# A causal attention with two expert layers behind it: joint transposes of the first keys, PReLU split between ScalarE and VectorE, low words in place

## The chip, the cores and the metric

The kernel runs on one core of a Trainium2 chip. The metric is the device time of one execution in microseconds (us). The kernel before takes 504.18 us (median of three runs, 503.7 to 505.47).

## What is computed

Everything is float32. A causal attention over 2 batches, 12 heads, 448 positions and 64 values a head, then two expert layers on its 896 x 768 output:

```python
scores = q @ k.T / 8; scores above the diagonal = -1e9
attn   = softmax(scores)                # exp(s - max), divided by (sum + 1e-9)
x      = (attn @ v)                     # heads side by side: 896 x 768
h      = x @ w_in                       # 768 -> 2048
y      = (max(h, 0) + alpha * min(h, 0)) @ w_out          # PReLU, 2048 -> 768
m      = max(max(y @ w1, y @ w2), y @ w3)                 # 768 -> 768
out    = m @ w_out2                     # 768 -> 768
```

## The kernel before

**Three products for one.** The expert layers multiply in a rounded 32-bit type. To keep float32's accuracy each operand is split into a high and a low part (`h`, `l`), and `product` (L403) issues three matmuls: high by high, low by high, high by low. All of them carry line 406: 2004 of the program's 2684 matmul records lie behind the attention.

**The weights arrive as 64-bit floats.** Class `Weights` (L301) loads 128 columns at a time as pairs of 32-bit words (`raw`) and makes float32 of them: ScalarE takes the size from the high word into `t` (`size`, L369) and scales the low word into a tile of its own, `r` (`low`, L387); VectorE clamps and shifts `t` (L373, L376), puts in the sign (`top`, L390) and adds `r` as integers (`both`, L401; a few on GpSimd); ScalarE then rounds the high part `wh` (L281) and VectorE or GpSimd subtracts for the low part `wl` (L293). `raw` has two buffers and is free again after `top`.

**Attention.** Twelve jobs, each of two heads (j = 0, 1) that share a batch. The 448 query rows are cut into four chunks c of 64, 128, 128 and 128 rows; chunk c sees 64, 192, 320 or 448 keys. A job runs: scores on TensorE (`ps`, L578) in two groups, chunks 3 and 0 and then 2 and 1; the mask and the row minimum of the negated scores on VectorE (L595); exponential and row sum on ScalarE (L608); the sums' reciprocals on VectorE (L619, L620); normalising on GpSimd (L624); transposes of the result on TensorE (`pt`, L643) in three banks a head: the first 64 keys (four transposes), keys of blocks 1 and 3 (four), keys of block 2 (two); a copy of each bank to SBUF (`p`, on VectorE or ScalarE, L287, L281); the product with v (`pv`, L652), the two heads in the two column halves of the array; and the split of its result into `xh` and `xl`.

**Order.** A planner (class `Plan`, L71) gives every step a rank, an estimated duration and a list of what must precede it, and writes out each engine's instructions in the order in which its own estimate would start them. Every engine then runs its list in order. While the attention runs, products of the first expert layer for the first batch's tokens (five blocks of 128 outputs, `NB`, ranks from `FILL_RANK`) are set between the attention's matmuls: they are called fillers here. 48 of their matmuls stand ahead of the last `pv`, 42 behind it.

**PReLU.** `prelu` (L670): VectorE takes alpha times the negative part from PSUM (L676), adds the positive part, also from PSUM (L686); ScalarE rounds the high part `g_h` (L281), VectorE subtracts for `g_l` (L293). The PSUM bank is free after the second VectorE instruction. Behind the attention seven banks serve these products.

**Start.** Eight matmuls on a tile of zeros (`warm`, L714) keep TensorE busy until the first q and k are there. The zeros are written by VectorE (L259).

Of the kernel before, what the change touches and what calls it, by code (L numbers as in the profile page):

```python
# [23 lines left out]
RINGS = dict(w=4, m=1, s=4, t=3, v=4, qk=3, e=3, p=4)  # L24
NB = 5
HELD = 4
WARM = 8
# [3 lines left out]
    load=-6, s=12, max=12, exp=16, recip=10,  # L31
# [6 lines left out]
FIRST = 0  # L38
SLACK = 0.02
# [31 lines left out]
class Plan:  # L71
# [27 lines left out]
    def add(  # L99
        self, rank, engines, fn, after=(), take=(), give=(), delay=0.0, port=False, mode="full"  # L100
    ):
# [6 lines left out]
        self.waiting[i] = (rank, engines, fn, after, tuple(take), give, delay, port, mode)  # L108
        self.open[i] = sum(d in self.waiting for d in after)
        for d in after:  # L110
            self.next.setdefault(d, []).append(i)
        if not self.open[i]:
            self.ready[i] = None
        return i

    def start(self, step):
# [12 lines left out]
        for engine, took in engines.items():  # L129
# [6 lines left out]
            if engine == "PE" and mode != self.mode:  # L136
# [9 lines left out]
    def run(self):  # L146
        while self.waiting:
# [20 lines left out]
            if engine == "PE":  # L168
                self.mode = mode
# [18 lines left out]
def attention_moe_moe2_kernel(  # L188
# [73 lines left out]
    mask = first.tile([P, S], F32, name="mask")  # L262
    nc.gpsimd.memset(mask, 0.0)
    nc.gpsimd.affine_select(
        out=mask[:, S - P :],
        in_=mask[:, S - P :],
        compare_op=ALU.is_ge,
        fill=FILL,
        base=0,
        pattern=[[-1, P]],  # L270
        channel_multiplier=1,
    )
    alpha_sb = const.tile([P, KF], F32, name="alpha_sb")
    nc.scalar.dma_start(out=alpha_sb, in_=alpha)
# [26 lines left out]
    class Weights:  # L301
# [3 lines left out]
        def __init__(self, rank, w, k0, n, f, parts=None, lo_engines=("DVE", "POOL"), after=()):  # L305
# [19 lines left out]
                rank, on_act(k, words=True), step(self.low), (load,), take=("cr",)  # L325
            )
            top = plan.add(
                rank, on_dve(k), step(self.top), (high, low), give=(("raw", load),), port=True
            )
            both = plan.add(  # L330
                rank, on_dve(k) | on_pool(k), self.both, (top, low), give=(("cr", low),), port=True
# [76 lines left out]
    class Product:  # L408


        def __init__(self, rank, pieces, bank, token):

            total = len(pieces)
            self.end = None
            for i, (count, n, terms, after, give) in enumerate(pieces):
                self.end = plan.add(
                    rank,
# [19 lines left out]
    BANKS = ((0,), (1, 3), (2,))  # L437
    AT_COL, BANK_COL = {}, [0]
# [7 lines left out]

    p_all = [at.tile([P, BANK_COL[-1]], F32, bufs=1, name=f"p{i}") for i in range(RINGS["p"])]
    for p in p_all:
        nc.vector.memset(p[ROWS[0] :, : BANK_COL[1]], 0.0)
# [4 lines left out]
    e_all = [at.tile([P, 2, NP], F32, bufs=1, name=f"e{i}") for i in range(RINGS["e"])]  # L454
    for e in e_all:
        nc.vector.memset(e[ROWS[0] :, :, : OFF[1]], 0.0)
    used = {"p": 0, "e": 0}
# [5 lines left out]
    class Job:  # L463


        def __init__(self, rank, b, hp):
            self.b, self.hp = b, hp
            self.ps, self.pt, self.p = {}, {}, {}

            def add(kind, *args, **kw):  # L470
# [3 lines left out]
            load_v = add("load", on_dma(256), step(self.load_v), take=("v",), delay=1.8)  # L474

            norm = [[], []]
            s = None
            for i, cs in enumerate(PAIRS):
# [7 lines left out]
                    give=(("qk", load_qk),) * (i == len(PAIRS) - 1),  # L486
# [21 lines left out]
                for c in cs:  # L508
                    for j in range(2):
                        took = on_pool(START[c + 1], two=False)  # L510
                        if b * HP + hp < FIRST:
                            took |= on_dve(START[c + 1], fast=True)
                        norm[j].append(
                            add("norm", took, partial(self.normalize, i, c, j), (r,), port=True)
# [3 lines left out]
            for j in range(2):  # L518
                for n in range(len(BANKS)):
                    w = BANK_COL[n + 1] - BANK_COL[n]  # L520
                    keys = sum(ROWS[kc] for kc in BANKS[n] for c in range(kc, NCH))
                    t = add(
                        "p",
                        {"PE": keys * 0.85e-3 + 0.03},
                        step(self.p_t, j, n),
                        norm[j] if t is None else [*norm[j], t],
                        take=("t",) + ("p",) * (n == 0),
                        give=(("e", e_took),) * (j == 1 and n == len(BANKS) - 1),
                    )
                    if n == 0:  # L530
                        p_took.append(t)
                    src = partial(self.pt.get, (j, n))
                    outs.append(
                        add(
                            "p_out",
                            on_dve(w, psum=True) | on_act(w, psum=True),
                            copy(partial(self.p_part, j, n), src),
                            (t,),
                            give=(("t", t),),
                        )  # L540
                    )
            a = add(
                "av",
                {"PE": 4 * BANK_COL[-1] / 2400},
# [3 lines left out]
                mode="columns",  # L548
# [464 lines left out]
```

## Time and profile before

| | |
|---|---|
| median of three runs | 504.18 us |
| the profiled execution | 504.13 us |
| its span, first to last instruction | 502.3 us |
| TensorE busy (PE) | 495.1 us, 99% |
| VectorE, ScalarE, GpSimd busy | 360.6, 256.9, 63.5 us |
| attention, to the last `pv` | 101.0 us |
| the rest, line 406 without a gap | 397.9 us |

In the profile PE is TensorE's matmuls, PEld its weight loads, DVE VectorE, ACT ScalarE, POOL GpSimd. A matmul record overlaps the next one, so its own duration says little: what one costs is the distance from its start to the next start. The granted TensorE clock is 1.00 (2.4 GHz) in every stretch shown below. A matmul in plain float32 (`ps`, `pv`) leaves two records, so 16 records of `pv` are the eight matmuls of one job.

### The profile page before, as it was taken

The page shows a single profiled execution, that of the slowest core. Times are in us where ns is not written, and L with a number is a line of the kernel's source. Part 1 is how long each engine was busy: PE and PEld are TensorE (multiplying, and loading weights), DVE is VectorE, ACT ScalarE, POOL GpSimd, SP SyncE. Part 2 cuts the span into 40 slices and gives each one's busy share as a digit, 9 for nine tenths or more (in the row PEclk, how much of TensorE's full clock was granted, in tenths as well). Part 3 has the DMA queues.
Part 4 walks back from the last instruction along what each step waited for, and adds up shares of the span by engine and source line. Part 5 has one row for each costly group of instructions (what it writes and reads, how often), then busy time and mean ns, then how long its engine had stood idle before and what let it go on. Part 6 is the DMA issues. An engine that isn't in the chain of part 4 may idle for free.

```text
span 502.3 us, 7218 instructions
## 1 busy us (share of the span) xinstructions
PE 495.1 (99%) x2684; PEld 427.5 (85%) x2684; DVE 360.6 (72%) x727; ACT 256.9 (51%) x502; POOL 63.5 (13%) x113
## 2 busy tenths in 40 slices
PE   8999999999999999999999999999999999999997
PEld 5665666789989899898899899898899899889997
DVE  7889878859999999968557467579999896601000
ACT  5999898645453555434425335366566544401111
POOL 3657755330100000000000000000000000000000
PEclk9999999999999999999999999999999999999999
DMA  7635410213332333333333343253554443000111
GB/s 255 234 88 173 154 44 13 111 67 125 127 126 78 112 127 105 116 115 106 115 116 104 93 138 122 69 185 128 188 186 160 157 134 118 1 1 31 64 64 63
DMA packets 14147, 56.70 MB, mean 113 GB/s; under 512 B 1696, under 2 KB 3488, under 8 KB 14112
## 3 DMA queue, kind: packets, MB, share of 16 engines
q1 hardware_dynamic: 13968, 56.24, 33.7%
q8 instruction: 21, 0.34, 0.3%
q14 instruction: 14, 0.11, 0.1%
q10 hardware_dynamic: 144, 0.01, 0.0%
HBM read 53.49 MB, written 2.75 MB: 112 GB/s over the span
## 4 chain that ended last, share of the span: by engine, by line
PE 94%; DVE 3%; ACT 2%; issue 0%; DVEq 0%
PE ps L406 81%; PE pt L643 4%; PE pv L652 4%; PE ps L578 4%; DVE e L595 2%; ACT e L608 1%; DVE sm L619 1%; PE warm L714 1%; DVE p L287 0%; ACT p L281 0%; DVE sm L620 0%; ACT o L281 0%; DVE nm L595 0%; ACT xh L281 0%; DVE zeros L259 0%
## 5 line engine op out<-in xcount | busy, mean ns | idle before, releaser
L406 PE MATMUL ps<-xh,wh 128*128 128x384 f32 (+2 forms) x408 | 149.4, 366 | 0.0
L406 PE MATMUL ps<-xh,wl 128*128 128x384 f32 (+2 forms) x408 | 148.7, 364 | 0.0
L406 PE MATMUL ps<-xl,wh 128*128 128x384 f32 (+2 forms) x408 | 148.5, 364 | 0.0
L406 PEld LDWEIGHTS ps<-xh,wh 128*128 128x128 f32 x408 | 76.7, 188 | 8.4 <-DVE xl L293 0.3
L406 PEld LDWEIGHTS ps<-xl,wh 128*128 128x128 f32 x408 | 76.6, 188 | 8.1
L406 PEld LDWEIGHTS ps<-xh,wl 128*128 128x128 f32 x408 | 76.5, 188 | 7.8
L281 ACT CAST wh<-t 128x768 fp32r<-128x768 f32 (+1 forms) x53 | 43.0, 811 | 73.3 <-DVE t L401 73.0
L406 PE MATMUL ps<-g_h,wl 128*128 128x512 f32 (+1 forms) x192 | 70.0, 365 | 0.0
L406 PE MATMUL ps<-g_l,wh 128*128 128x512 f32 (+1 forms) x192 | 69.9, 364 | 0.0
L406 PE MATMUL ps<-g_h,wh 128*128 128x512 f32 (+1 forms) x192 | 69.6, 362 | 0.0
L369 ACT ACTIVATE t<-raw 128x768 f32<-128x768 f32 (+1 forms) x59 | 52.3, 887 | 14.0 <-DMA raw<-in_moe_w_dram 5.0
L293 DVE TENSOR_TENSOR wl<-t,wh 128x768 fp32r<-128x768 f32 (+1 forms) x47 | 43.3, 921 | 21.9 <-ACT wh L281 21.9
L390 DVE SCALAR_TENSOR_TENSOR t<-raw,t 128x768 uint32<-128x768 uint32 (+1 forms) x59 | 54.7, 927 | 0.9
L401 DVE CUSTOM_DVE_ANT_0 t<-t,r 128x1536 uint16<-128x1536 uint16 (+1 forms) x57 | 52.6, 924 | 2.2
L387 ACT ACTIVATE r<-raw 128x768 uint32<-128x768 uint32 (+1 forms) x59 | 52.0, 881 | 4.1 <-DMA raw<-in_moe_w_dram 3.1
L608 ACT ACTIVATE e<-e,nm 128x448 f32<-128x448 f32 (+3 forms) x96 | 47.8, 503 | 5.1 <-DVE nm L595 4.9
L624 POOL TENSOR_SCALAR e<-e,sm 128x448 f32<-128x448 f32 (+3 forms) x96 | 45.6, 494 | 31.2 <-DVE sm L620 12.5
L406 PEld LDWEIGHTS ps<-g_l,wh 128*128 128x128 f32 x192 | 36.0, 188 | 4.1
L406 PEld LDWEIGHTS ps<-g_h,wh 128*128 128x128 f32 x192 | 36.1, 188 | 4.1
L406 PEld LDWEIGHTS ps<-g_h,wl 128*128 128x128 f32 x192 | 36.0, 188 | 3.8
L281 ACT CAST g_h<-g 128x512 fp32r<-128x512 f32 (+2 forms) x32 | 18.1, 567 | 39.2 <-DVE g L686 39.0
L595 DVE CUSTOM_DVE_ANT_0 e<-ps,mask 128x448 f32<-128x448 f32 (+3 forms) x96 | 35.2, 413 | 4.1 <-PE ps L578 3.9
(53 smaller groups left out, 584.0 us busy)
## 6 DMA issues: line engine op xcount, KB each, us to landing
raw<-in_moe_w_dram SPq DMA_DIRECT2D x18, 768.0 KB, 4.3
raw<-in_moe_w_in_dram SPq DMA_DIRECT2D x17, 768.0 KB, 4.4
raw<-in_moe_w_out_dram SPq DMA_DIRECT2D x12, 768.0 KB, 4.4
raw<-in_moe_w_out_dram SPq DMA_DIRECT2D x12, 640.0 KB, 4.1
qk<-in_qk_dram SPq DMA_DIRECT2D x12, 448.0 KB, 3.5
v<-in_v_dram SPq DMA_DIRECT2D x12, 256.0 KB, 2.7
out_dram<-o SPq DMA_DIRECT2D x14, 192.0 KB, 1.9
alpha_sb<-in_moe_alpha_dram ACTq DMA_DIRECT2D x1, 8.0 KB, 3.5
```

The lines of the kernel that those rows point to most:

```text
L281: nc.scalar.copy(out(), src())
L293: ENGINE[engine].tensor_tensor(out=out(), in0=a(), in1=f32(b()), op=ALU.subtract)
L369: nc.scalar.activation(out=f32(self.t), in_=f32(self.raw[..., 1]), func=AF.Abs)
L387: nc.scalar.activation(out=self.r, in_=self.raw[..., 0], func=AF.Copy, scale=2.0**-29)
L390: nc.vector.scalar_tensor_tensor(out=self.t, in0=self.raw[..., 1], scalar=0xC0000000, in1=self.t, op0=ALU.bitwise_and, op1=ALU.bitwise_or,)
L401: ENGINE[engine].tensor_tensor(out=t, in0=t, in1=self.r.bitcast(I32), op=ALU.add)
L406: nc.tensor.matmul(ps, a, c, start=(first and y == 0), stop=(last and y == 2))
L578: nc.tensor.matmul(ps, self.qk[d, 0, START[c] : START[c] + P], self.qk[d, 1, :n], start=True, stop=True,)
L595: nc.vector.tensor_tensor_reduce(out=self.e_part(c, j), in0=self.ps[c, j], in1=mask[: ROWS[c], m - n : m], op0=ALU.add, op1=ALU.min, scale ...
L608: nc.scalar.activation(out=s, in_=s, func=AF.Exp, scale=-1.0, bias=self.column(self.nm, i, c, j), accum_out=self.column(self.sm, i, c, j),)
L624: ENGINE[engine].tensor_scalar(out=s, in0=s, scalar1=self.column(self.sm, i, c, j), scalar2=1.0, op0=ALU.mult, op1=ALU.mult,)
L643: nc.tensor.transpose(pt[:keys, o : o + P], self.e[:, j, s : s + keys], ident)
```

## The change

1. **Joint transposes.** Head 0's keys are reversed on the host, so that its first 64 keys stand last in each row of the probabilities, right ahead of head 1's first 64 keys. One 128 x 128 transpose then covers both heads' first keys. v's first rows are laid out as one 128 x 128 block, zero where a row belongs to the other head, so the first matmul of `pv` takes both heads at once on the whole array, and six on column halves follow. Banks per job go from six to five: key block 2 (two transposes) and key blocks 1 and 3 (four) for each head, then the joint one (four), which is last and needs both heads.
2. **First job.** Its scores come in three groups, chunks 1 and 0, then 2, then 3.
3. **PReLU behind the attention.** ScalarE reads the PSUM bank twice, relu(-h) into `n` and relu(h) into `g`; VectorE joins them, `g - alpha * n`. The bank is free after ScalarE's second reading; `n` has one buffer. The five products of the early tokens keep the old form.
4. **Low words in place.** ScalarE writes the scaled low words over the raw low words; the integer addition reads them there, every second word; `raw` is free after the addition.
5. **Order behind the attention.** The two token blocks (512 and 384) alternate: each weight block begins with the token block that the one before it ended with, and the pieces of w_out are taken weight by weight.
6. **Small.** Nine warming matmuls on a constant instead of eight on zeros; two masks; alpha is loaded by SyncE instead of ScalarE's queue, and VectorE negates it once; four memsets of `p` are gone.

```diff
-RINGS = dict(w=4, m=1, s=4, t=3, v=4, qk=3, e=3, p=4)
+RINGS = dict(w=4, m=1, s=4, t=3, v=4, qk=3, e=3, p0=2, p=4)
-WARM = 8
+WARM = 9
-    plan.buffers(**RINGS, raw=2, ct=2, cr=2, eg=2)
-    zeros = first.tile([P, S], mybir.dt.bfloat16, name="zeros")
-    nc.vector.memset(zeros, 0.0)
+    plan.buffers(**RINGS, raw=2, ct=2, eg=2, en=EN)
+    ones = nc.const_aps.tensor(1.0, [P, S], mybir.dt.bfloat16)
...
         def low(self):
-            self.r = wcvt.tile([P, KC, P], U32, tag="r", name="r")[:, : self.n]
-            nc.scalar.activation(out=self.r, in_=self.raw[..., 0], func=AF.Copy, scale=2.0**-29)
+            low = self.raw[..., 0]
+            nc.scalar.activation(out=low, in_=low, func=AF.Copy, scale=2.0**-29)
...
-            ENGINE[engine].tensor_tensor(out=t, in0=t, in1=self.r.bitcast(I32), op=ALU.add)
+            ENGINE[engine].tensor_tensor(out=t, in0=t, in1=self.raw[..., 0].bitcast(I32), op=ALU.add)
...
-    BANKS = ((0,), (1, 3), (2,))
+    BANKS = ((2,), (1, 3))
...
+            self.groups = ((1, 0), (2,), (3,)) if rank == 0 else PAIRS
...
-            for j in range(2):
-                for n in range(len(BANKS)):
+            parts = [(j, kcs) for j in range(2) for kcs in BANKS] + [(0, (0,))]
+            for j, kcs in parts:
...
-                    s = OFF[c] + START[kc]
-                    o = AT_COL[kc] - BANK_COL[n] + START[c] - START[kc]
-                    nc.tensor.transpose(pt[:keys, o : o + P], self.e[:, j, s : s + keys], ident)
+                    o = AT_COL[kc] - AT_COL[kcs[0]] + START[c] - START[kc]
+                    s = 2 * OFF[c] + START[c + 1] + (START[kc] if j else -START[kc + 1])
+                    nc.tensor.transpose(pt[:, o : o + P], self.e[:, s : s + P], ident)
...
-            for kc in range(NCH):
+            nc.tensor.matmul(
+                pv, self.v[:, 0].rearrange("p j d -> p (j d)"), self.p0, start=True, stop=False
+            )
+            for kc in range(1, NCH):
...
+        def parts():
+            o["n"] = epi.tile([P, BANK], F32, tag="n", bufs=EN, name="n")[:, :N]
+            o["g"] = epi.tile([P, BANK], F32, tag="g", name="g")[:, :N]
+            nc.scalar.activation(out=o["n"], in_=prod.ps[:, :N], func=AF.Relu, scale=-1.0)
+            nc.scalar.activation(out=o["g"], in_=prod.ps[:, :N], func=AF.Relu)
+        def join():
+            nc.vector.scalar_tensor_tensor(
+                out=o["g"], in0=o["n"], scalar=minus_alpha[:, f : f + 1], in1=o["g"],
+                op0=ALU.mult, op1=ALU.add,
+            )
```

Where the instructions stand now. On TensorE, the first job's scores and transposes in the kernel before (`ps` scores, `pt` transposes; x2 means twice in a row):

```order
17 L578 MATMUL ps<-qk 128x448 x2
18 L578 MATMUL ps<-qk 128x64 x2
19 L578 MATMUL ps<-qk 128x320 x2
20 L578 MATMUL ps<-qk 128x192 x2
...
27 L578 MATMUL ps<-qk 128x320 x2
28 L578 MATMUL ps<-qk 128x192 x2
29 L643 MATMUL pt<-ident,e_126 64x128 x4
30 L643 MATMUL pt<-ident,e_126 128x128 x6
31 L643 MATMUL pt<-ident,e_126 64x128 x4
32 L643 MATMUL pt<-ident,e_126 128x128 x6
33 L578 MATMUL ps<-qk 128x448 x2
```

and now:

```order
19 L612 MATMUL ps<-qk 128x192 x2
20 L612 MATMUL ps<-qk 128x64 x2
21 L612 MATMUL ps<-qk 128x320 x2
22 L612 MATMUL ps<-qk 128x448 x4
...
26 L612 MATMUL ps<-qk 128x448 x2
27 L612 MATMUL ps<-qk 128x64 x2
28 L681 MATMUL pt<-ident,e_121 128x128 x6
29 L612 MATMUL ps<-qk 128x320 x2
30 L612 MATMUL ps<-qk 128x192 x2
31 L681 MATMUL pt<-ident,e_121 128x128 x10
```

The first group has 256 columns a head instead of 512, and the first job issues 16 transposes (6 and 10) where it issued 20; the first six stand ahead of the third job's second group of scores. On TensorE, a product with v and what stands around it in the kernel before (fourth job):

```order
86 L578 MATMUL ps<-qk 128x448 x2
87 L578 MATMUL ps<-qk 128x64 x2
88 L652 MATMUL pv<-p_113,v 64x448
89 L652 MATMUL pv<-p_115,v 64x448
90 L652 MATMUL pv<-p_113,v 64x384
```

and now (fourth job):

```order
70 L612 MATMUL ps<-qk 128x448 x2
71 L612 MATMUL ps<-qk 128x64 x2
72 L691 MATMUL pv<-p_571,v 128x448
73 L696 MATMUL pv<-p,v 64x384 x2
74 L696 MATMUL pv<-p,v 64x256 x2
75 L696 MATMUL pv<-p,v 64x128 x2
76 L681 MATMUL pt<-ident,e_122 128x128 x4
```

Seven matmuls instead of eight; the first fills the whole array, so the change to column halves falls inside the product. On ScalarE, in the stage of w_in, the kernel before has

```order
183 L369 ACTIVATE t<-raw 128x768
184 L387 ACTIVATE r<-raw 128x768
185 L281 CAST g_h<-g 128x512
186 L281 CAST g_h<-g 128x384
187 L281 CAST wh<-t 128x768
```

and the same stretch now:

```order
218 L399 ACTIVATE t<-raw 128x768
219 L417 ACTIVATE raw<-raw 128x768
220 L311 CAST g_h<-g 128x512
221 L737 ACTIVATE n<-ps 128x512
222 L738 ACTIVATE g<-ps 128x512
223 L311 CAST g_h<-g 128x384
224 L311 CAST wh<-t 128x768
225 L737 ACTIVATE n<-ps 128x384
226 L738 ACTIVATE g<-ps 128x384
```

ScalarE has five instructions for a weight block before and nine now. Up to the last `pv` the TensorE list holds 240 transposes and 48 fillers before, 192 and 30 now; the numbers of matmuls on line 406 over the whole program are the same.

## Rows read from the trace of the kernel before

**Rows 1.** Page: busy us by engine.
```profile
PE 495.1 (99%) x2684; PEld 427.5 (85%) x2684; DVE 360.6 (72%) x727; ACT 256.9 (51%) x502; POOL 63.5 (13%) x113
```
**Rows 2.** The closing chain in order of time: start us, us, what.
```profile
1.15 3.17 PE warm L714 x8
4.32 1.77 PE ps L578 x8
...
101.03 397.94 PE ps L406 x2004
```
**Rows 3.** Timeline of PE, one job's turn: start us, us, instruction, records.
```profile
28.75 2.43 PE L643 MATMUL pt<-ident,e 128*128 128x128 f32 x20
31.11 1.19 PE L578 MATMUL ps<-qk 64*128 64x448 f32 x8
32.23 2.27 PE L652 MATMUL pv<-p,v 128*64 128x448 f32 x16
34.43 0.44 PE L643 MATMUL pt<-ident,e 128*128 128x128 f32 x2
34.79 1.13 PE L578 MATMUL ps<-qk 64*128 64x320 f32 x8
35.86 1.73 PE L643 MATMUL pt<-ident,e 128*64 128x128 f32 x14
```
**Rows 4.** Stretches of 0.05 us, the product with v alone: us, busy PE, PEld, DVE, ACT.
```profile
32.65:32.70 0.05, 0.05 (x4) 0.04 (x2) 0.00 (x0) 0.00 (x0) 1.00 0.00 0
...
33.00:33.05 0.05, 0.05 (x4) 0.02 (x2) 0.00 (x0) 0.00 (x0) 1.00 0.00 0
```
**Rows 5.** Timeline of PE, a product with v behind fillers.
```profile
98.26 0.36 PE L406 MATMUL ps<-xl,wh 128*128 128x448 f32 x1
98.46 0.37 PE L406 MATMUL ps<-xh,wl 128*128 128x448 f32 x1
98.76 2.27 PE L652 MATMUL pv<-p,v 128*64 128x448 f32 x16
```
**Rows 6.** Timeline of PE: the two longest gaps inside the attention, in brackets.
```profile
50.06 0.44 PE L643 MATMUL pt<-ident,e 128*128 128x128 f32 x2 [0.52 <-DVE p L287]
...
62.30 0.44 PE L643 MATMUL pt<-ident,e 128*128 128x128 f32 x2 [0.73 <-DVE p L287]
```
**Rows 7.** Stretches: us, busy PE, PEld, DVE, ACT, POOL, clock, DMA, GB/s.
```profile
25.00:50.00 25.00, 24.55 (x184) 15.65 (x184) 22.35 (x88) 23.96 (x77) 16.74 (x31) 1.00 0.42 130
...
130.00:200.00 70.00, 70.00 (x349) 63.06 (x348) 68.35 (x108) 34.58 (x49) 0.17 (x1) 1.00 0.33 109
```
**Rows 8.** Groups by line: the copies of the transposed banks, busy us, mean ns.
```profile
L281 ACT COPY p<-pt 64x448 f32<-64x448 f32 (+2 forms) x39 | 18.9, 506 | 6.0 <-PE pt L643 5.4
L287 DVE COPY p<-pt 128x256 f32<-128x256 f32 (+2 forms) x33 | 17.8, 553 | 7.4 <-PE pt L643 7.1
```
**Rows 9.** Timeline of ACT: the first job's first and last exponential.
```profile
6.86 0.67 ACT L608 ACTIVATE e<-e,nm 128x448 f32<-128x448 f32 x1 [4.40 <-DVE nm L595]
...
10.37 0.44 ACT L608 ACTIVATE e<-e,nm 128x192 f32<-128x192 f32 x1
```
**Rows 10.** Groups by line and shape from 130 to 200 us.
```profile
L401 DVE CUSTOM_DVE_ANT_0 t<-t,r 128x1536 uint16<-128x1536 uint16 x10 | 9.5, 950 | 0.0
L390 DVE SCALAR_TENSOR_TENSOR t<-raw,t 128x768 uint32<-128x768 uint32 x10 | 9.5, 950 | 0.0
...
L676 DVE TENSOR_SCALAR g<-ps,alpha_sb 128x512 f32<-128x512 f32 x9 | 6.7, 747 | 0.0
L686 DVE SCALAR_TENSOR_TENSOR g<-ps,g 128x512 f32<-128x512 f32 x9 | 6.2, 684 | 0.0
...
L676 DVE TENSOR_SCALAR g<-ps,alpha_sb 128x384 f32<-128x384 f32 x8 | 4.9, 612 | 0.0
```
**Rows 11.** Groups by line: copies from PSUM by ScalarE, and the low words.
```profile
L387 ACT ACTIVATE r<-raw 128x768 uint32<-128x768 uint32 (+1 forms) x59 | 52.0, 881 | 4.1 <-DMA raw<-in_moe_w_dram 3.1
...
L281 ACT COPY m<-ps 128x512 f32<-128x512 f32 (+1 forms) x11 | 5.9, 535 | 8.0 <-PE ps L406 7.9
```

More of the change, by code (lines that the diff above doesn't have):

```diff
@@ L38 @@
 FIRST = 0
+EN = 1
 SLACK = 0.02
@@ L99, in add @@
     def add(
-        self, rank, engines, fn, after=(), take=(), give=(), delay=0.0, port=False, mode="full"
+        self,
+        rank,
+        engines,
+        fn,
+        after=(),
+        take=(),
+        give=(),
+        delay=0.0,
+        port=False,
+        mode="full",
+        leaves=None,
     ):
@@ L107, in add @@
         after = tuple(dict.fromkeys(after))
-        self.waiting[i] = (rank, engines, fn, after, tuple(take), give, delay, port, mode)
+        self.waiting[i] = (rank, engines, fn, after, tuple(take), give, delay, port, (mode, leaves or mode))
         self.open[i] = sum(d in self.waiting for d in after)
@@ L324, in __init__ @@
             low = plan.add(
[L325 removed]
+                rank, on_act(k, words=True), step(self.low), (load,)
             )
             top = plan.add(
[L328 removed]
+                rank, on_dve(k), step(self.top), (high, low), port=True
             )
             both = plan.add(
[L331 removed]
+                rank, on_dve(k) | on_pool(k), self.both, (top, low), give=(("raw", load),), port=True
             )
@@ L512, in __init__ @@
                             took |= on_dve(START[c + 1], fast=True)
-                        norm[j].append(
-                            add("norm", took, partial(self.normalize, i, c, j), (r,), port=True)
+                        norm[c, j] = add(
+                            "norm", took, partial(self.normalize, i, c, j), (r,), port=True
                         )
             t, outs, p_took = None, [], []
-            for j in range(2):
-                for n in range(len(BANKS)):
[L520 to L528, printed above, removed]
-                    )
[L530 to L541, printed above, removed]
@@ new lines, in __init__ @@
+            parts = [(j, kcs) for j in range(2) for kcs in BANKS] + [(0, (0,))]
+            for j, kcs in parts:
+                w = sum(S - START[kc] for kc in kcs)
+                heads = (0, 1) if 0 in kcs else (j,)
+                ring = "p0" if 0 in kcs else "p"
+                first = 0 in kcs or kcs == BANKS[0]
+                done = [norm[c, h] for c in range(min(kcs), NCH) for h in heads]
+                t = add(
+                    "p",
+                    {"PE": sum(NCH - kc for kc in kcs) * 0.11 + 0.03},
+                    step(self.p_t, j, kcs),
+                    done if t is None else [*done, t],
+                    take=("t",) + (ring,) * first,
+                    give=(("e", e_took),) * (0 in kcs),
+                )
+                if first:
+                    p_took.append((ring, t))
+                outs.append(
+                    add(
+                        "p_out",
+                        on_dve(w, psum=True) | on_act(w, psum=True),
+                        copy(partial(self.p_part, j, kcs), partial(self.pt.get, (j, kcs))),
+                        (t,),
+                        give=(("t", t),),
+                    )
+                )
@@ L547, in __init__ @@
                 take=("t",),
-                mode="columns",
-                give=(*(("p", x) for x in p_took), ("v", load_v)),
+                give=(*p_took, ("v", load_v)),
+                leaves="columns",
             )
@@ L713, in warm @@
         for _ in range(WARM):
-            nc.tensor.matmul(ps, zeros[:, :P], zeros, start=True, stop=True)
+            nc.tensor.matmul(ps, ones[:, :P], ones, start=True, stop=True)
     plan.add(0, {"PE": WARM * 0.36}, step(warm), take=("m",), give=(("m", None),))
```

171 lines of the change are left out of this document (108 added, 63 removed).

## Prediction

> **What bounds the kernel now.** I read the page's busy times first, then the chain that ended last, then TensorE's timeline inside the attention, then the busy time of all engines by stretch. The reader should see in the first that TensorE's matmuls cover 495.1 of 502.3 us [rows 1], and in the second that the last 397.94 us ahead of the output are line 406 alone, 2004 records without a gap [rows 2]. The number of these matmuls does not change, so no faster VectorE or ScalarE shortens that part: it can only move forward as a block, or be torn open. What can shrink lies ahead of 101.03 us. There TensorE is busy too: 24.55 of 25 us, with ScalarE at 23.96 and VectorE at 22.35 [rows 7]. The two longest gaps, 0.52 and 0.73 us, end with VectorE's copy of a transposed bank [rows 6]. So the attention is TensorE's, with the other two close behind.
>
> The profiled execution took 504.13 us for a span of 502.3, 0.05 below the median of 504.18; the sum is made on 504.13, and the difference is left out.
>
> **The change part by part.**
>
> *Transposes.* 48 of 240 go (12 jobs, four each). Twenty transposes take 31.11 - 28.75 = 2.36 us from first start to the next instruction, two take 34.79 - 34.43 = 0.36 [rows 3]; the difference gives 2.00 / 18 = 0.111 us each, and 2.36 / 20 = 0.118 with the entry counted. 48 x 0.111 = **-5.3 us**, at most -5.7. A 64-key transpose counts like the others: the run of twenty holds eight of them, the run of two none.
>
> *The product with v.* A job's product takes 34.43 - 32.23 = 2.20 us [rows 3]. Its records run in twos: where two end two others start, at about 32.67 and 33.02, 0.35 us apart for 448 columns of both heads [rows 4]. The joint matmul streams 448 columns once over the whole array, so by these rows it takes as long as the pair that it replaces: no gain. What is new is the change from the whole array to column halves inside the product. Behind fillers, which use the whole array, `pv` starts 98.76 - 98.46 = 0.30 us after the last matmul, where fillers follow each other at 0.20 [rows 5]: 0.10 for that change. Scores with a `pv` behind them take 32.23 - 31.11 = 1.12 us, with transposes behind them 35.86 - 34.79 = 1.07, at 512 columns a head both times [rows 3]: coming from the scores, the whole array is 0.05 cheaper to enter than the halves. Before, nine products follow scores and three follow work on the whole array; now twelve change inside. 12 x 0.10 - 3 x 0.10 - 9 x 0.05 = **+0.45 us**. Bounds: below, -0.45 (the inner change is free); above, an entry and an exit for each of the twelve: two transposes between `pv` and scores take 0.36 where 2 x 0.111 = 0.22 would do, so 0.14 + 0.10 = 0.24, and 2.9 us.
>
> The Trainium skill ("TensorEngine Tiling", section Key Properties) says that changing the tiling mode drains the TensorE. The trace agrees that a change costs something, 0.05 to 0.14 us. By that rule at its dearest the sum would lie 2.4 us higher; that is a rival below.
>
> *Copies.* Each job copies one 448-column bank fewer. A copy is 0.506 us on ScalarE, 0.553 on VectorE [rows 8]: 12 x 0.53 = 6.4 us less, about 3.2 on each of the two engines that stand close behind TensorE. This is not in the sum; it is what lets the -5.3 count. TensorE's job shortens from 6.9 us (2.36 and 2.20 and twice about 1.1) by 0.4, the other two by 0.27 each.
>
> *First job.* Its first group of scores shrinks from 512 to 256 columns a head, and that group took 1.77 us [rows 2], so VectorE and ScalarE may begin some 0.9 us earlier. ScalarE then runs without a long break from 6.86 us on, through the first job's last exponential at 10.37 [rows 9]; begun earlier, it ends earlier by about the same, minus two more reciprocals on VectorE. Nine warming matmuls instead of eight add 3.17 / 8 = 0.40 us, but need no zeros from VectorE, for which TensorE waited till 1.15 [rows 2]: taken as zero together. I take **-0.8 us**; bounds 0 (eaten by the second job) and -1.5.
>
> *Gaps in the attention.* With TensorE 0.4 us faster a job, the lists of three engines fit closer. Before, the two longest gaps make 1.25 us [rows 6]. I take as much again, **+1.25 us**; bounds -1.25 (they close, since the copies are fewer) and +4.
>
> *PReLU.* From 130 to 200 us VectorE is busy 68.35 of 70 us and ScalarE 34.58 [rows 7], over ten weight blocks (the integer addition x10 [rows 10]): 6.84 and 3.46 us a block, where TensorE takes 7.0. Both VectorE instructions on PSUM, 0.747 and 0.684 us [rows 10], become one on SBUF; leaving out the first alone saves 0.747 + 0.612 = 1.36 us a block, so VectorE falls to 5.5. ScalarE gets four readings of PSUM at about 0.535 [rows 11], 2.1 us: 5.6 of 7.0. Both fit, TensorE had no gap there before, so **0**. Its cover is TensorE's 7.0 us and the seven banks.
>
> The Trainium skill ("ScalarE: Activation LUTs", section Rules for kernel authors) gives relu to VectorE. The rows disagree for PSUM: ScalarE reads 512 columns in 0.535 us, VectorE in 0.684 to 0.747. By the rule as by the rows the sum gains nothing, but by the rule ScalarE would be the one to watch here.
>
> *Low words in place.* ScalarE reads the words at this stride already, 0.881 us [rows 11]; no row shows it writing so: between 0 and 0.9 us more for each of 59. The addition takes 0.950 us, and so does `top`, which reads its words at the same stride [rows 10]; I take 0 by that row, and at worst twice the time. `raw` is free one addition, 0.95 us, later, which two buffers and 7.0 us a block absorb. **0**.
>
> *Order, alpha.* The alternating blocks exchange equal matmuls: 0. Alpha's small load now queues on SyncE behind eight loads of q, k and v; its first reader is a filler's PReLU, far behind the first jobs: 0.
>
> Sum: 504.13 - 5.3 + 0.45 - 0.8 + 1.25 = **499.7 us**.
>
> **The rivals.**
>
> 1. *ScalarE and VectorE bound the attention*, so TensorE's 5.3 us turn into waits and only the copies count: -3.2 us and nothing for the start, 501.0. For it: ScalarE at 23.96 of 25. Against: the two together are 46.3 of 50, with weight conversion among it that is not urgent.
> 2. *Each inner change of tiling drains at the dearest price*: 2.4 us above the forecast, 502.1. Against it are the 0.10 of rows 5.
> 3. *The strided second source halves the addition's rate*: up to 0.85 us more for each of 59. Five or six of them lie in the attention: 5 us on VectorE, of which ScalarE can take half over: 502.2. Behind it VectorE has 7.0 - 5.5 = 1.5 us a block to spare.
> 4. *The three lists no longer mesh* (slots, banks, GpSimd's late normalising): gaps of 5 to 6 us in place of 1.25, 504.
> 5. *Slower: ScalarE and VectorE take turns in the w_in stage.* `n` has one buffer, so ScalarE's next reading waits for VectorE's join, behind which stand weight steps that themselves wait for ScalarE. Run one after the other, 5.6 + 5.5 = 11.1 us a block against 7.0. Some five free banks, 3.5 us of products each, cover 18 us; over eleven blocks the stage bears 7.0 + 18 / 11 = 8.6 us. From there on TensorE stops; at 9.5 us a block it loses 11 x 0.9 = 10 us: 499.7 + 10 = 510; at 9.1 about 505. Against it: ScalarE's list puts weight steps of a different block between, and before, VectorE ran 98% full without a stop of TensorE.
>
> That the transposes would not go is excluded by the order: 192 are listed.
>
> **How the numbers follow.** Forecast 0.62, rival 1 0.14, rival 2 0.06, rival 3 0.06, rival 4 0.06, rival 5 0.06. The forecast's own bounds: -5.7, -0.45, -1.5, -1.25 together would give 495.2, and all upper ends 506; terms seldom all lean one way, so 497.3 to 502. Rivals 1 to 3 reach to 502.2; with part of rival 4 the range is **497.3 to 502.8**. 0.3%, about what a measurement can tell here from no change, is 1.5 us: faster is below 502.67. That holds for the forecast but a few hundredths, for rival 1 almost wholly, for half of rivals 2 and 3: 0.82. Within: half of rivals 2 and 3, rival 4 and a little of 5: 0.11. Slower: 0.07.
>
> **What would show it.** In the profile after: the last `pv` ends near 92 us (18 fillers fewer ahead of it, 3.7 us, and the 4.4 gained), and line 406 follows without a gap, some 3.7 us longer; a gap there is rival 5. Runs of transposes at 0.11 us each. A `pv` of 2.2 to 2.35 us; 2.45 is rival 2. The first exponential near 6 us. The addition at 0.95 us; 1.8 is rival 3. ScalarE full and TensorE with many short gaps from 15 to 50 us is rival 1. I am wrong if the attention's end moves by less than the fillers' 3.7 us, or if the block of line 406 opens.

## The result and the profile after

The kernel after takes 509.84 us (median of six runs, 509.23 to 511.83) against 504.19 for the one before in the same measurement: 1.0119 times the time, interval 1.0097 to 1.0142. It is slower; the prediction said 499.7, faster, within 497.3 to 502.8. The profiled execution took 511.32 us, its span is 509.5; it is one of the slower two of the six, whose mean granted clock is 0.993, where the four near the median have 0.995 to 0.997.

The chain of the kernel after that ended last, from the last product with v on (start us, us, what), answers to [rows 2]:

```profile
91.72 1.45 PE pv L696 x12
93.16 26.24 PE ps L436 x128
119.42 0.83 ACT wh L311
...
126.12 0.95 DVE wl L323
128.91 22.20 PE ps L436 x104
151.13 0.84 ACT wh L311
152.00 0.96 DVE wl L323
155.29 0.87 DVE t L420
159.34 346.84 PE ps L436 x1746
```

The attention did what was forecast: its last `pv` ends at 93.16 us instead of 101.03, with 30 fillers ahead of it instead of 48. But the block behind it, one piece of 397.94 us before, is now in three pieces. From 93.16 to its end at 506.18 (159.34 + 346.84) it takes 413.0 us. With the 18 fillers that moved behind the attention (18 x 0.2035 = 3.7 us) it should take 401.6.

TensorE's timeline at the gaps (start us, us, instruction, idle time before it in brackets and what ended it):

```profile
122.30 0.50 PE L436 MATMUL ps<-xh,wl 128*128 128x512 f32 x1 [1.26 <-DVE wl L323]
...
125.84 0.39 PE L436 MATMUL ps<-xh,wl 128*128 128x512 f32 x1
128.91 0.74 PE L436 MATMUL ps<-xh,wh 128*128 128x448 f32 x1 [2.69 <-DVE g L751]
129.45 0.57 PE L436 MATMUL ps<-xl,wh 128*128 128x448 f32 x1
129.82 0.57 PE L436 MATMUL ps<-xh,wl 128*128 128x448 f32 x1
...
154.68 0.34 PE L436 MATMUL ps<-xh,wl 128*128 128x384 f32 x1
159.34 0.74 PE L436 MATMUL ps<-xh,wh 128*128 128x448 f32 x1 [4.32 <-DVE g L751]
```

Two waits, 2.69 us and the 4.3 that end at 159.34, are for line 751, the second half of the old PReLU: it frees the fillers' only PSUM bank. TensorE's starts show the price: three distances are longer than the pace allows, by 1.42, 2.84 and 4.49 us, together 8.75. Behind the two long ones 17 matmuls come at nearly twice their distance (448 columns at 0.37 instead of 0.20) and cost another 3.2. Four single distances elsewhere, three of them around the wait of 1.26 us, add 0.6. That makes 12.6 us.

ScalarE's and VectorE's timelines of the kernel after show what was late:

```profile
119.42 0.83 ACT L311 CAST wh<-t 128x768 fp32r<-128x768 f32 x1 [5.77 <-PE ps L436]
...
134.21 0.84 ACT L311 CAST wh<-t 128x768 fp32r<-128x768 f32 x1 [2.96 <-PE ps L436]
...
151.13 0.84 ACT L311 CAST wh<-t 128x768 fp32r<-128x768 f32 x1 [3.81 <-PE ps L436]
```

```profile
120.76 0.62 DVE L323 TENSOR_TENSOR g_l<-g,g_h 128x448 fp32r<-128x448 f32 x1 [5.79 <-ACT g_h L311]
...
152.00 0.96 DVE L323 TENSOR_TENSOR wl<-t,wh 128x768 fp32r<-128x768 f32 x1 [2.68 <-ACT wh L311]
...
157.55 0.67 DVE L725 TENSOR_SCALAR g<-ps,alpha_sb 128x448 f32<-128x448 f32 x1
158.14 0.60 DVE L741 SCALAR_TENSOR_TENSOR g<-n,minus_alpha,g 128x384 f32<-128x384 f32 x1
158.67 0.61 DVE L751 SCALAR_TENSOR_TENSOR g<-ps,g 128x448 f32<-128x448 f32 x1
```

ScalarE stands for 5.77 us before it may round a block's high part: `wh` has no free slot until TensorE has finished an older block. From 93 to 165 us there are four such waits, 16.6 us in all; before there were 0.3 us in the whole run. VectorE stands behind ScalarE, the fillers' PReLU stands behind VectorE's weight steps, and TensorE stands behind that PReLU.

**Whose slots.** The ring `w` has four slots. W0 to W4 are the five filler blocks of w_in; W1 to W4 are held, each keeps its slot until its early tokens' fillers and its late tokens' product are both done. In the planner's account a held slot comes back with the late product alone (`give` of the last of `us`), though fillers of that block may come after it. Read from the order of TensorE's instructions, the filler pieces of W3 are spread until W9's products in the kernel after, those of W4 until W11's, three matmuls between 18. The six pieces of one block add up in the bank, and nothing is emptied between them. The 18 come from the planner: it allows 0.12 us (`SAME`) between two pieces of one product and starts another product there. With one bank the fillers of only one block are open at a time, so it is always a late product that comes between. This reason is read from the code; no run changes it. W6, W8 and W10 come into the slot that W5, W6 and W8 have just left. For W6 0.6 us of matmuls lie between the slot's release and its first use there; before, the shortest such stretch was 9.1 us. This stretch is the number that the expectations below use.

### The profile page after: what moved, and what is told of

It reads as the page before. It is cut to its first block, busy times and chain, and to the rows that moved or that the text cites. A ratio compares the mean times of both kernels' runs of the same rounds, so it can differ in the third digit from the quotient of the medians.

```text
span 509.5 us, 7143 instructions
## 1 busy us (share of the span) xinstructions
PE 495.2 (97%) x2613; PEld 425.1 (83%) x2613; DVE 347.5 (68%) x697; ACT 274.1 (54%) x548; POOL 59.1 (12%) x112
## 4 chain that ended last, share of the span: by engine, by line
PE 90%; DVE 5%; ACT 3%; issue 1%; ACTq 0%; DVEq 0%
PE ps L436 78%; PE ps L612 4%; PE pt L681 3%; PE pv L696 3%; ACT e L643 2%; PE pv L691 1%; DVE e L630 1%; PE warm L786 1%; DVE sm L655 1%; ACT p L311 1%; DVE wl L323 1%; DVE t L420 1%; DVE g L741 0%; DVE p L317 0%; ACT wh L311 0%
## 5 line engine op out<-in xcount | busy, mean ns | idle before, releaser
L436 PEld LDWEIGHTS ps<-xh,wh 128*128 128x128 f32 x408 | 77.5, 190 | 16.6 <-DVE g L751 7.8
L431 DVE CUSTOM_DVE_ANT_0 t<-raw,t 128x1536 uint16<-128x1536 uint16 (+1 forms) x58 | 53.7, 925 | 3.3 <-DVE t L420 0.5
L417 ACT ACTIVATE raw<-raw 128x768 uint32<-128x768 uint32 (+1 forms) x59 | 52.6, 891 | 0.0
L643 ACT ACTIVATE e<-e,nm 128x192 f32<-128x192 f32 (+3 forms) x96 | 47.8, 502 | 6.1 <-DVE nm L630 5.9
L660 POOL TENSOR_SCALAR e<-e,sm 128x192 f32<-128x192 f32 (+3 forms) x96 | 46.0, 498 | 28.2 <-DVE sm L656 19.1
L630 DVE CUSTOM_DVE_ANT_0 e<-ps,mask 128x192 f32<-128x192 f32 (+3 forms) x96 | 35.7, 413 | 7.3 <-PE ps L612 6.9
L403 DVE TENSOR_SCALAR t<-t 128x768 f32<-128x768 f32 (+1 forms) x59 | 32.0, 543 | 7.3 <-ACT t L399 6.1
```

Source lines behind the costliest of these rows:

```text
L403: nc.vector.tensor_scalar(out=f32(t), in0=f32(t), scalar1=LEAST, scalar2=MOST, op0=ALU.max, op1=ALU.min)
L417: nc.scalar.activation(out=low, in_=low, func=AF.Copy, scale=2.0**-29)
L431: ENGINE[engine].tensor_tensor(out=t, in0=t, in1=self.raw[..., 0].bitcast(I32), op=ALU.add)
L436: nc.tensor.matmul(ps, a, c, start=(first and y == 0), stop=(last and y == 2))
L630: nc.vector.tensor_tensor_reduce(out=self.e_part(c, j), in0=self.ps[c, j], in1=masks[j][: ROWS[c], m : m + n], op0=ALU.add, op1=ALU.min, s ...
L643: nc.scalar.activation(out=s, in_=s, func=AF.Exp, scale=-1.0, bias=self.column(self.nm, i, c, j), accum_out=self.column(self.sm, i, c, j),)
```

## The experiments

Theory A at the outset: the faster attention leaves 60 fillers behind it, these hold slots, and the late cast follows. Theory B is the prediction's fifth rival: the split PReLU makes ScalarE and VectorE take turns. Kernels of one group shared the runs of the kernel before.

| run | fillers ahead / behind the last `pv` | us | ratio, 95% interval |
|---|---|---|---|
| after | 30 / 60 | 509.84 | 1.0119, 1.0097 to 1.0142 |
| e1 old PReLU | 30 / 60 | 511.94 | 1.0152, 1.0138 to 1.0166 |
| e2 three held | 30 / 42 | 498.36 | 0.9884, 0.9871 to 0.9898 |
| e3 fillers first | 30 / 60 | 506.18 | 1.0038, 1.0024 to 1.0052 |
| e4 before, six blocks | 48 / 60 | 509.04 | 1.0097, 1.0083 to 1.0111 |
| e5 slots kept | 30 / 60 | 509.81 | 1.0110, 1.0090 to 1.0131 |
| e6 before, three held | 48 / 24 | 504.42 | 1.0001, 0.9992 to 1.0009 |
| e7 three held, old PReLU | 30 / 42 | 498.33 | 0.9884, 0.9869 to 0.9898 |
| e8 three held, joint alone | 33 / 39 | 500.02 | 0.9920, 0.9907 to 0.9932 |
| e9 five slots, old PReLU | 30 / 60 | 509.06 | 1.0096, 1.0082 to 1.0110 |
| e10 three held, fixed order | 30 / 42 | 501.53 | 0.9945, 0.9932 to 0.9959 |
| e11 three held, old pairs | 33 / 39 | 498.72 | 0.9890, 0.9877 to 0.9904 |
| e12 free banks | 30 / 60 | 498.87 | 0.9897, 0.9883 to 0.9910 |
| e13 before, six, free banks | 48 / 60 | 504.53 | 1.0006, 0.9997 to 1.0015 |
| e14 free banks, fixed order | 30 / 60 | 499.79 | 0.9917, 0.9903 to 0.9930 |

### e1: the old PReLU

```diff
-            prelu(rank, prod, u, f, lambda: room["late_g"], "b", True)
+            prelu(rank, prod, u, f, lambda: room["late_g"], "b", False)
```

> The kernel after, with the PReLU behind the attention in its old form (two VectorE reads of PSUM) and all else of the change kept. Theory A (slots: the faster attention leaves 60 filler products instead of 42 behind the last pv, these hold the weight slots of their blocks, and W6 is cast into the slot that W5 has just left, 0.6 us of TensorE time ahead of its first use): slots and order of TensorE are as in the kernel after, so ScalarE's cast of W6 still waits some 5 us or more for TensorE, TensorE still has gaps of several us between 93 and 165 us, time 507 to 511. Theory B (ScalarE and VectorE take turns at the PReLU through the one buffer n, and this opens the gaps): the gaps go, time 498.5 to 500.5.

511.94 us, the gaps are there (2.64 us ahead of 127.94, for line 751 again), ScalarE's cast waits 19.7 us for TensorE between 93 and 170 us. Theory B falls. In a torn block the new form is 2.1 us the better one by the medians, though the two intervals overlap.

### e2: three held blocks

```diff
-NB = 5
-HELD = 4
+NB = 4
+HELD = 3
```

> The kernel after, with one filler block less (NB 4, HELD 3; PReLU in the new form). Fillers ahead of the last pv stay 30, those behind it fall from 60 to 42, and the smallest stretch of TensorE time between the release of a weight slot and the first use of the next block in it goes from 0.6 to 9.1 us. Theory A (slots): no gaps of TensorE over 0.3 us behind the attention, ScalarE's cast waits for TensorE under 1 us in all, 498.5 to 500.5, faster than the kernel before by 0.7 to 1.1%. Theory B (the PReLU's turns): the late PReLUs are as before this edit, the gaps stay, 505 to 510.

498.36 us. The chain behind the attention is one piece again:

```profile
92.67 400.45 PE ps L436 x2022
```

The cast's waits for TensorE fall to one of 1.6 us. The loss is in what is left over of the fillers; what they lose, slots or something else, this run does not tell.

### e3: fillers ahead of the next blocks

```diff
+        fill_end = prod.end
...
-            after = w.ready + [j.done for j in jobs]
+            after = w.ready + [j.done for j in jobs] + ([] if NB - HELD <= f < NB else [fill_end])
```

> The kernel after, in which the products of the blocks that are not held wait until the last filler product has been issued; 60 fillers still stand behind the last pv and the PReLU keeps its new form. Smallest stretch between a slot's release and the first use of its next block: 13.4 us. Theory A (slots): no gap over 0.3 us from late casts; 498.5 to 500.5, or up to 503 if the single PSUM bank of the fillers then sets their pace. Theory B (the PReLU's turns): gaps stay, 505 to 510. A third, C (60 fillers on one bank are the loss by themselves, whatever the slots do): TensorE waits for the VectorE PReLU of a filler at each of the three to four fillers left, 502 to 506.

506.18 us, just above theory C's range. TensorE's timeline shows the gaps (of the profiled execution, 508.89 us):

```profile
116.04 0.74 PE L436 MATMUL ps<-xh,wh 128*128 128x448 f32 x1 [2.99 <-DVE g L751]
...
124.84 0.48 PE L436 MATMUL ps<-xh,wh 128*128 128x448 f32 x1 [2.18 <-DVE g L751]
```

Where one block's fillers follow the other's with nothing between, TensorE waits while VectorE empties the single bank.

### e4: one filler block more in the kernel before

```diff
-NB = 5
+NB = 6
```

> The kernel before, untouched but for one filler block more (NB 6, four held): 48 fillers stay ahead of the last pv and 60 stand behind it, as in the kernel after. Smallest stretch between a slot's release and the first use of its next block: 0.6 us, at W7, then 8.4 and 4.9 us. Theory A (slots): the gaps of the kernel after appear without any of its other edits: ScalarE's cast waits several us for TensorE, 509 to 516. Theory B (the PReLU's turns): the PReLU is the old one, no gaps, 503.5 to 505.5.

509.04 us: the kernel before, without a single edit of the change, loses 4.5 us by one filler block more (504.5 in the same measurement). Its cast waits 11.8 us for TensorE, 6.8 at the longest, and TensorE stands again for the second half of the PReLU (L686 here):

```profile
127.26 0.83 ACT L281 CAST wh<-t 128x768 fp32r<-128x768 f32 x1 [6.81 <-PE ps L406]
```

```profile
135.85 0.47 PE L406 MATMUL ps<-xh,wh 128*128 128x448 f32 x1 [1.78 <-DVE g L686]
```

So the loss needs no edit of the change but its by-product, 60 fillers behind the attention.

### e5: an honest account of the slots

```diff
-                    (("w", w.took),) * (u == us[-1]),
+                    (("w", w.took),) * (u == us[-1] and w not in held),
...
+        if w in held:
+            both = [prod.end, fill_end[f]]
+            plan.add(rank, {"PE": 0.0}, step(lambda: None), both, give=(("w", w.took),))
```

> The kernel after with all its edits and its five filler blocks (30 filler products ahead of the last pv, 60 behind it); only the planner's account is changed: a held block gives its weight slot back when both its second late product and its last filler product have been issued, not at the late product alone. Smallest stretch between release and first use of the next block: 7.3 us of TensorE time (W6), 13.4 and more from W7 on, against 0.6. Theory A (the early account of the slots is the loss): ScalarE's cast waits under 2 us for TensorE, 498.5 to 502, where up to 3 us may be lost because fillers of two blocks now stand one behind the other on their single bank. Theory C (60 fillers behind the attention are the loss by themselves): 504 to 510. Theory B (the PReLU's turns): 505 to 510.

509.81 us: theory A's forecast failed. The cast no longer waits for TensorE between 93 and 180 us, but the gaps are others: two of 1.97 and 2.18 us for line 751, where fillers now stand one behind the other, and then two for a block that is converted late:

```profile
121.76 0.47 PE L436 MATMUL ps<-xh,wh 128*128 128x448 f32 x1 [1.97 <-DVE g L751]
129.40 0.47 PE L436 MATMUL ps<-xh,wh 128*128 128x448 f32 x1 [2.18 <-DVE g L751]
```

```profile
151.51 0.50 PE L436 MATMUL ps<-xh,wh 128*128 128x512 f32 x1 [2.18 <-ACT wh L311]
...
153.24 0.50 PE L436 MATMUL ps<-xh,wl 128*128 128x512 f32 x1 [0.99 <-DVE wl L323]
```

### e6 to e8: whose gain is it

```diff
 e6, kernel before:  NB = 4, HELD = 3
 e7, from e2:        prelu(rank, prod, u, f, lambda: room["late_g"], "b", False)
 e8, from e7:        self.groups = PAIRS, and the sequences in the old order (e10)
```

> The kernel before with NB 4 and HELD 3 alone: 48 filler products ahead of the last pv, 24 behind it, smallest stretch of a slot 15.7 us. It tells whether the gain of the run with three held blocks comes from the attention or from this setting. Theory A: the kernel before had no gap of TensorE behind the attention to lose, so 503.7 to 504.7, no change, and the 6 us of the three-held run belong to the attention's edits. Rival (fewer held blocks are a gain by themselves): 500 to 503.

> The kernel after with NB 4 and HELD 3 (498.36 us), and the PReLU behind the attention in its old form, two VectorE reads of PSUM. Slots as in that run. Theory A and my forecast (the PReLU's form costs and gains nothing while TensorE has no gap): 498.0 to 498.8. Rival (VectorE at 1.0 share of 101 to 200 us in the old form becomes the bound once the attention ends earlier): 499.5 to 501. Theory B (the split costs turns that the three-held run still pays): below 497.9.

> The kernel after with NB 4 and HELD 3, without the PReLU split, without the to-and-fro order of sequences and with the first job's scores in the old pairs; the joint transposes, the order of the transposes, alpha's load on SP, the warm tile of constants and the low words in place remain. 33 fillers stand ahead of the last pv. My terms for the parts left out: PReLU 0, order 0, first job 0.8 us. So 498.4 + 0.8 less the 3 fillers that then stand ahead (0.6 us, paid behind otherwise): 498.4 to 499.4. Rival (the order or the PReLU carries part of the gain): 500 to 502.

504.42, 498.33 and 500.02 us. Fewer held blocks are no gain by themselves, so e2's 6 us are the change's. The PReLU's form is worth nothing while TensorE has no gap: e7 and e2 differ by 0.03. e8 lies 1.7 us behind e2, above my 499.4: one of the terms that I had at 0 does not seem to be 0.

### e9: a fifth slot

```diff
-RINGS = dict(w=4, m=1, s=4, t=3, v=4, qk=3, e=3, p0=2, p=4)
+RINGS = dict(w=5, m=1, s=4, t=3, v=4, qk=3, e=3, p0=2, p=4)
```

with e1's edit, against which it is to be read.

> The kernel after with the PReLU in its old form throughout (511.94 us in the first experiment) and a fifth weight slot, which fits in the room of the buffer n. The order of TensorE is the same piece by piece: 30 fillers ahead of the last pv, 60 behind it, spread between the products of W5 to W12. Smallest stretch between release and first use of a slot: 9.1 us instead of 0.6. Theory A (the slots that W2 to W4 still hold are the loss): no gap over 0.3 us behind the attention, 498 to 500. Theory C (60 fillers on their single PSUM bank are the loss by themselves): the gaps stay, 504 to 512.

509.06 us, 2.9 less than e1, with the intervals apart: the slot is worth something, but most of the loss stays. Theory A as I had put it falls, and the shortest stretch is no measure of the loss (9.1 us here and in e2). ScalarE's timeline shows why a slot more does not cure it:

```profile
119.80 0.83 ACT L311 CAST wh<-t 128x768 fp32r<-128x768 f32 x1 [5.31 <-PE ps L436]
```

The cast is now needed later, but it stands in ScalarE's list where the planner believed a slot free, and everything behind it waits all the same.

### e10 and e11: the order, and the first job

```diff
 e10, from e2
-        return [(u, cut[u]) for u in (range(len(cut)) if i % 2 == 0 else reversed(range(len(cut))))]
+        return [(u, cut[u]) for u in range(len(cut))]
 (and the pieces of w_out and the slots' release as before)
 e11, from e2
-            self.groups = ((1, 0), (2,), (3,)) if rank == 0 else PAIRS
+            self.groups = PAIRS
```

> The three-held version (498.36 us) with the sequences in the old fixed order: the to-and-fro edit alone undone. My term for it was 0: 498.1 to 498.7. Rival (it carries the 1.6 us by which the run without order, PReLU split and first-job edit was behind): 499.5 to 500.3.

> The three-held version (498.36 us) with the first job's scores in the old pairs: that edit alone undone. My term for it was 0.8 us: 498.9 to 499.5, first exp near 6.9 us instead of 6. Rival (the whole 1.6 us is here): 499.7 to 500.3; rival (hidden by the fillers, of which 33 then stand ahead): 498.1 to 498.6.

501.53 and 498.72 us. The first job is worth 0.4 us net by the medians (forecast 0.8, less 0.6 for three fillers more behind the attention), which lies within the spread of the two (498.06 to 498.79 and 498.05 to 499.22). The order is worth 3.2, forecast 0. Part of it is again the fillers' bank:

```profile
125.43 0.47 PE L436 MATMUL ps<-xh,wh 128*128 128x448 f32 x1 [1.44 <-DVE g L751]
```

### e12 to e14: the fillers behind the attention on free banks

```diff
-        prod = Product(r, pieces, lambda: ps_m.tile([P, BANK], F32, tag="m", name="ps"), "m")
-        prelu(r + RANK["prelu"], prod, SEQ[0], f, lambda: early_g, "m", False)
+        tok = "b" if f >= 3 else "m"
+        own = bank if f >= 3 else lambda: ps_m.tile([P, BANK], F32, tag="m", name="ps")
+        prod = Product(r, pieces, own, tok)
+        prelu(r + RANK["prelu"], prod, SEQ[0], f, lambda: early_g, tok, False)
 (and `room` and `bank` are defined ahead of the loop)
```

Only blocks from W3 on take the free banks; the fillers of W1 and W2 that stand behind the attention keep the one bank. e12 is the kernel after with this alone, e13 the kernel before with six blocks (e4) and the same, e14 is e12 in the old order.

> The kernel after with all its edits, five filler blocks, four slots and the early account; alone the filler products of W3 and W4, which all stand behind the last pv, take a bank of the seven that the attention leaves free instead of the one bank m. 30 fillers stay ahead of the last pv and 60 behind it, but they now end within about 20 us of it, and the slots come free (smallest stretch 14.7 us). Theory D (the one bank spreads the 60 fillers over 65 us behind the attention; they hold three of the four slots so long, casts of new blocks come to stand in ScalarE's list ahead of their slot's release, and all that is behind waits): no gap over 0.3 us, 498 to 499.5. Theory C' (60 fillers cost by their number, for their old PReLU on VectorE or their casts on ScalarE, on whichever bank): 503 to 510.

> The kernel before with six filler blocks (509.04 us), and the fillers behind the attention on the seven free banks. 60 fillers behind the last pv as there; smallest stretch 11.5 us. Theory D: back to the kernel before, 503.5 to 504.7. Theory C': 507 to 510.

> The kernel after with the fillers of W3 and W4 on free banks, and the to-and-fro order undone. If the 3.1 us that the order was worth with three held blocks came of one late cast (the cast at 120.7 us and the gap of 1.4 us behind it), nothing is left of them here: as the run with free banks within 0.5 us, 498 to 499.5. If the order is a gain by itself, in the stages from 200 us on: 501 to 502.

498.87, 504.53 and 499.79 us. With 60 fillers left, four slots and the early account, the loss is gone from both kernels: 11 us from the kernel after, 4.5 from e4. The chain behind the attention and the stretches of e12 (us, busy PE, PEld, DVE, ACT, POOL, clock, DMA, GB/s), with those of the kernel after below:

```profile
93.18 400.53 PE ps L436 x2022
```

```profile
101.00:130.00 29.00, 29.00 (x144) 26.38 (x143) 23.41 (x36) 17.33 (x29) 0.00 (x0) 1.00 0.24 82
130.00:165.00 35.00, 35.00 (x176) 31.54 (x175) 31.26 (x47) 26.52 (x46) 0.00 (x0) 1.00 0.33 113
```

```profile
101.00:130.00 29.00, 24.96 (x117) 21.47 (x116) 20.32 (x31) 17.04 (x28) 0.00 (x0) 0.98 0.24 82
130.00:165.00 35.00, 30.68 (x143) 27.58 (x142) 25.79 (x40) 19.52 (x34) 0.00 (x0) 0.92 0.27 91
```

In e12 the last filler stands ahead of W6's products and its PReLU runs at 128.4 us, 35 us behind the attention (I had expected 20); in the kernel after the last runs at 183.0, 90 us behind. ScalarE's cast does not wait for TensorE once in e12. So the root is the fillers' one bank. With it the fillers of one block alone are open, so that 60 of them are spread over the stage, where in e12's list those of W3 stand between those of W2; as long as they are spread they hold slots, and the cast comes too late (after, e1, e4, e9); pushed together, they wait while the bank is emptied (e3, e5). More slots, an honest account or another order each treat one of the two and leave the other.

e14 settles the order: without any gap it is still 0.9 us behind e12. Its chain behind the attention is 401.63 us for the same 2022 records, e12's 400.53. From the starts of all records from 94 us on, 512 columns are followed by 512 after 0.2292 us on average in e14 and 0.2283 in e12, 384 by 384 after 0.1745 and 0.1741; times some 780 and 1030 this is the 1.1 us. So of e10's 3.2 us about 1 is the order's own, the gap took 1.4, the attention's end 0.4. With the first job's 0.4 the order's 1 accounts for e8 too, but for 0.3. Why a matmul follows a little sooner in the alternating order was not tried.

## Why the prediction was wrong

**The step that failed** is the one on which the whole prediction rested: that the block of line 406 moves forward as it stands. It was written twice, as "Both fit, TensorE had no gap there before, so **0**. Its cover is TensorE's 7.0 us and the seven banks" and as "line 406 follows without a gap, some 3.7 us longer". I counted the 18 displaced fillers as 3.7 us of matmuls and did not ask which resources they need behind the attention. They do not use the seven banks; they use one. And of the four slots on which a conversion every 7.0 us depends, three are theirs until they are done. In the kernel before, 42 fillers just fitted (e6: with 24 nothing is gained), 60 do not (e4). The measured price is 413.0 - 400.5 = 12.5 us against e12 in the profiled executions, 11.0 by the medians.

The text said that a gap there would be rival 5. It is not: the place and the size were that rival's (510 us), the mechanism was not (e1), so that its figure was met by luck.

The other steps, with the block whole (e2, e12: 498.36 and 498.87 against 499.7 forecast):

- *Attention.* Its end is 7.9 us earlier, less 3.7 for the fillers: 4.2 gained, forecast 4.4. (The "near 92 us" of the prediction does not follow from its own terms: 101.03 - 4.4 - 3.7 is 92.9.)
- *Product with v.* Forecast 0.45 us, measured 1.4. TensorE's timeline of the kernel after, a product behind scores and one behind transposes:

```profile
28.81 1.19 PE L612 MATMUL ps<-qk 64*128 64x448 f32 x8
29.93 1.02 PE L691 MATMUL pv<-p,v 128*128 128x448 f32 x2
30.88 1.51 PE L696 MATMUL pv<-p,v 128*64 128x384 f32 x12
32.33 0.44 PE L681 MATMUL pt<-ident,e 128*128 128x128 f32 x2
...
84.48 0.60 PE L681 MATMUL pt<-ident,e 128*128 128x128 f32 x4
84.92 0.92 PE L691 MATMUL pv<-p,v 128*128 128x448 f32 x2
85.77 1.52 PE L696 MATMUL pv<-p,v 128*64 128x384 f32 x12
87.21 0.44 PE L681 MATMUL pt<-ident,e 128*128 128x128 f32 x2
```

  and the one behind transposes in the kernel before:

```profile
92.13 0.60 PE L643 MATMUL pt<-ident,e 128*128 128x128 f32 x4
92.66 2.27 PE L652 MATMUL pv<-p,v 128*64 128x448 f32 x16
94.86 0.44 PE L643 MATMUL pt<-ident,e 128*128 128x128 f32 x2
```

  Scores and product take 3.52 us (28.81 to 32.33) instead of 3.32 [rows 3]. Four transposes and product take 2.73 both times, and behind fillers the time is the old one too. Seven of twelve stand behind scores now: 7 x 0.20 = 1.4 us. That scores are cheaper to leave for the whole array, from which I took 0.45 off, did not show. A change of tiling costs time here, as the Trainium skill ("TensorEngine Tiling (Array Packing)", section Key Properties) has it: 0.20 us where the way from scores to column halves has one change more, and nothing where the change from the whole array only moved from ahead of the product into it.
- *Gaps in the attention.* From 12 to 93 us TensorE waits 0.7 us instead of 1.6: 0.9 gained, where 1.25 more had been forecast.
- *First job and transposes.* The first exponential stands at 6.11 us, forecast 6; the edit is worth 0.4 net (e11, not clear of its spread), forecast 0.2. With the two terms above, 4.2 + 1.4 - 0.9 = 4.7 us are left for this edit and the transposes in the attention, forecast 6.1: three misses that nearly cancel, which is luck. From start to start, waits left out, the transposes up to the last `pv` take 24.2 us instead of 28.8, so most of the 4.7 is theirs (4.6, forecast 5.3) and the first job gave little.
- *PReLU.* 0, as forecast (e7).
- *Low words in place.* 0, as forecast. The addition in the kernel before, busy us and mean ns:

```profile
L401 DVE CUSTOM_DVE_ANT_0 t<-t,r 128x1536 uint16<-128x1536 uint16 (+1 forms) x57 | 52.6, 924 | 2.2
```

  The groups of the kernel after, the second against 881 of [rows 11]:

```profile
L431 DVE CUSTOM_DVE_ANT_0 t<-raw,t 128x1536 uint16<-128x1536 uint16 (+1 forms) x58 | 53.7, 925 | 3.3 <-DVE t L420 0.5
...
L417 ACT ACTIVATE raw<-raw 128x768 uint32<-128x768 uint32 (+1 forms) x59 | 52.6, 891 | 0.0
```

  (924 and 925 are means over both shapes, 950 in [rows 10] was that of the larger one.) Rival 3 is out.
- *Order.* Forecast 0, measured 1 us gained. This term was put at 0 and is not; it is why the versions without a gap lie below the forecast.

e2 and e12 beat both kernels, by 1.2% and 1.0% of the kernel before.

## What to carry to other kernels

Work that is moved is not only time: ask which bank, slot or buffer it occupies at the new place, and until when, and count it there. A block without a gap in the profile says nothing of how near it is to one; one block of fillers more in the kernel before would have shown that it had hardly any reserve. When a stage falls apart, give the suspect resource more room in the old kernel and in the new, and trust the remedy that works in both.

## What was not expected of the hardware

After TensorE's gaps of 2.69 and 4.3 us the next matmuls ran at little more than half pace, and the granted clock is 0.61 and 0.56 in the stretches of 3 us in which they start: means of a time mostly at the lower of its two levels, 1.2 GHz, where before and after it is 2.4.

```profile
128.00:131.00 3.00, 2.09 (x6) 1.96 (x7) 3.00 (x6) 2.64 (x5) 0.00 (x0) 0.61 0.04 15
...
159.00:162.00 3.00, 2.66 (x7) 2.24 (x8) 2.77 (x5) 2.53 (x6) 0.00 (x0) 0.56 0.60 240
```

Behind the gaps of 1.26 us (after, at 122.30) and 1.44 (e10) the pace stayed as it was. The clock fell as well in e4, e9 and e5, where gaps of 1.78, 2.03 and 2.18 us end at 135.85, 126.73 and 129.40 us; e4's row:

```profile
137.00:140.00 3.00, 3.00 (x12) 3.00 (x11) 3.00 (x5) 1.03 (x2) 0.00 (x0) 0.55 0.11 20
```

So the two long gaps of the kernel after cost 3.2 us more than their own length, a quarter of the whole loss in the profiled execution.
